# A fifth staging buffer, another order of stores and wider pieces in the background weight preparation of a fused attention and mixture-of-experts kernel

## The chip, the cores and the metric

The program runs on one core of one Trainium2 chip, as one launch. The metric is device time in microseconds: the median of several runs without the profiler. Beside it stands one profiled execution, whose trace gives the rows below.

## The reference, cut to what matters

```python
# x1 = attention(q, k, v): 4 x 8 heads, 576 positions, head size 64, causal window of 64,
#      laid out as 2304 tokens x 512
def _moe_ref(x, w_gate, w1, w2):            # dense: all 8 experts on all tokens
    P = np.exp(x @ w_gate - ...)            # then 8 rounds of row and column scaling
    for e in range(8):
        out += P[:, e:e+1] * (np.maximum(x @ w1[e], 0) @ w2[e])    # 512 -> 1024 -> 512
def _moe2_ref(x, w_gate, w1, w2):           # routed: each token goes to one expert, 288 per expert
    for e in range(8):
        mask = assigned == e
        out[mask] = np.maximum(x[mask] @ w1[e], 0) @ w2[e]
```

The output is `_moe2_ref(_moe_ref(attention))`, in float32.

## The kernel before

Matrix products with weights run in float16 with two halves: a float32 value is written as a high half and a low half, and three products (high-high, high-low, low-high) are summed in PSUM. The halves of a weight have to be made on the chip. ScalarE (ACT) makes the high half with one scaled copy and VectorE (DVE) makes the low half as the difference (`split_f`, lines 345 and 347). That pair is called a split here: 512 columns, 128 partitions.

The program has three parts. First, attention over 18 tiles of 128 tokens, together with the first expert of the dense layer; here the instruction order comes from a planner, `Flow`, with estimated costs, and the flag `bg.hold` is true. Second, experts 1 to 7 of the dense layer in a written-out order: `layer1s` and `layer2s` run one level of Strassen's scheme, seven products for each pair of token tiles, nine pairs for each expert. Third, the routed layer: `route`, `ffn` and `put`.

While the second part runs, `weights_all` prepares weights in the background, job after job. A job loads one float32 weight matrix (2 MB, in four quarters) into the one buffer `raw` (`load`, line 1621), computes its scale from sums of squares (`sum_scale`, line 287 on ACT, line 302 on TensorE), and makes splits. Each split goes into a buffer named `st2k`, of which there are 4, and from there by DMA into a scratch tensor in HBM, from which later stages load it: `w1scr` (`strassen_w1`, line 427, 14 splits), `w2scr` (`quarters_w2`, line 533, 14 splits, and `prep_w2`, line 498), `ws` for the routed layer (`prep_moe2`, line 473, 8 splits). These stores are issued by GpSimd (POOL). There are 31 jobs. When a quarter of `raw` is no longer needed, `free(r)` issues the load of the same quarter for the next job on SyncE (SP).

The pace of the background is counted in units. `layer1s` and `layer2s` call `bg.tick(0, DT / 2)` twice in each product, with DT = 1.4, so a product advances the background by 1.4 units. Before a split the job waits SPW units, and between its high and low half LOW = 0.7 units. After the load of a quarter is issued, its squares are not put into the instruction order before 11 units have passed (`bg.ready`). The order of instructions on each engine is fixed by this when the program is built; on the chip an engine that has to wait holds everything behind it.

In `strassen_w1` the seven outputs are made in the order A22, A11, A12, S1, S2, S3, S4, and then all four quarters of `raw` are freed. S4 is a sum written over A12 by DVE (line 414).

For expert 1 alone, `quarters_w2` runs during attention, with `bg.hold` true; its 14 splits use four slices of `acc` as buffers instead of `st2k`, and are stored by POOL as well. During attention SP also issues the loads of q, k and v for tiles ahead, and POOL also runs the reductions of `largest_v` over partitions.

In the last dense expert, `held_gate` uses a tile `xT2` for a transposed row block, and `rc["y"]` holds the scaled results that POOL adds into `acc` by DMA (line 1085).

Of the kernel before, what the change touches and what calls it, by code (L numbers as in the profile page):

```python
# [8 lines left out]
F32 = mybir.dt.float32  # L9
# [5 lines left out]
PSUM = bass.MemoryType.PSUM  # L15
M2PLAN = {1: 2, 2: 2, 3: 2, 4: 3, 5: 2, 6: 3, 7: 2}
DT = 1.4
SPW = 1.2
LOW = 0.7
MANE, MANP = 1, 1  # L20
PR = (4, 0)
# [154 lines left out]
def body(ctx, tc, dims, q, k, v, wg1, w11, w12, wg2, w21, w22, wgT, out):  # L176
# [154 lines left out]
    w2flat = [w2b[:, o:o + 4096] for o in (0, 4096)]  # L331
    w2v = [t.rearrange("p (c f) -> p c f", c=FC) for t in w2flat]

    def st2k():
        return rc["pool"].tile([128, 1040], F16, name="st2k", bufs=4)

    def wsc():
        return small.tile([128, 1], F32, name="wsc", bufs=3)
# [38 lines left out]
    def strassen_w1(e, sc, free):  # L377
        wr = raw.rearrange("p (c f) -> p c f", c=DC)
        hf = F // 2
        A11, A12 = wr[:, 0:2, 0:hf], wr[:, 2:4, 0:hf]  # L380
        A21, A22 = wr[:, 0:2, hf:], wr[:, 2:4, hf:]

        def sp(src, name):
            for c in range(2):
                yield from split_f(src[:, c], wq[name][0][:, c], wq[name][1][:, c], sc, 512, wait=1.2 if e == 1 else 1.8)

        if e == 1:
            t3 = acc[:, NT - 2:]

            def comb(dst, x, y, op):  # L390
                yield Rq("DVE", 1.2, wait=1.5)
                V.tensor_tensor(dst, x, y, op)

            yield from comb(t3, A11, A21, OP.subtract)
            yield from comb(A21, A21, A22, OP.add)
            while "T" not in rc:
                yield IDLE
            yield from sp(t3, "S3")
            yield from comb(t3, A21, A11, OP.subtract)
            yield from sp(t3, "S2")  # L400
            yield from comb(t3, A12, t3, OP.subtract)
            while ("l1", e - 1) not in bg.done:
                yield IDLE
            yield from sp(A21, "S1")
            yield from sp(A11, "A11")
            yield from sp(A12, "A12")
            yield from sp(A22, "A22")
            yield from sp(t3, "S4")
        else:
            t3 = rc["tmp"]  # L410

            def comb(dst, x, y, op):
                yield Rq("DVE", 1.2, wait=1.5)
                V.tensor_tensor(dst, x, y, op)

            def out(src, name):
                o = W1N.index(name) * 2048
                for c in range(2):
                    st = []

                    def two():
                        st.append(st2k()[:, 0:1024].rearrange("p (t x) -> p t x", t=2))
                        return st[0][:, 0], st[0][:, 1]

                    yield from split_f(src[:, c], two, None, sc, 512, wait=SPW)
                    d = w1scr[e * 128:(e + 1) * 128, o:o + 2048].rearrange("p (t x) -> p t x", t=2)
                    G.dma_start(d[:, :, c * 512:(c + 1) * 512], st[0])

            yield from comb(t3, A11, A21, OP.subtract)
            yield from out(A22, "A22")  # L430
            yield from comb(A21, A21, A22, OP.add)
            yield from out(A11, "A11")
            yield from comb(A11, A21, A11, OP.subtract)
            yield from out(A12, "A12")
            yield from comb(A12, A12, A11, OP.subtract)
            for n, q in ((A21, "S1"), (A11, "S2"), (t3, "S3"), (A12, "S4")):
                yield from out(n, q)
            bg.done.add(("w1p", e))
        for r in range(4):
            free(r)  # L440
        if e == 1:
            bg.done.add(("w1", e))

    W1N = ("A11", "A12", "S2", "S1", "S3", "S4", "A22")
# [15 lines left out]
    def prep_moe2(e, m, free):  # L460
        sc = wsc()
        yield from sum_scale(raw, winv[:, 2 + m, e:e + 1], sc, "job")
        for c in range(8):
            a, cc = (c % 2, c // 2) if m == 0 else (c // 4, c % 4)
            st = []

            def two():
                st.append(st2k()[:, 0:1024].rearrange("p (t x) -> p t x", t=2))
                return st[0][:, 0], st[0][:, 1]

            x, y = yield from split_f(raw[:, c * 512:(c + 1) * 512], two, None, sc, 512, pool="st2k", wait=SPW if c else 1.0)
            d = wscr[m][a][e * 128:(e + 1) * 128, :].rearrange("p (t x) -> p t x", t=2)
            G.dma_start(d[:, :, cc * 512:cc * 512 + 512], st[0])  # L473
            fl.release("st2k", x.idx, y.end + 4.6)
            if c % 2:
                free(c // 2)
# [7 lines left out]
    def w2rows(e):  # L484
        return w2scr[e * 128:(e + 1) * 128, 0:2 * FC * DM].rearrange("p (t x) -> p t x", t=2)

    def prep_w2(e, free):
        yield from sum_scale(raw, winv[:, 1, e:e + 1], w2sc, "job")
        for c in range(8):
            cs = slice(c * 512, (c + 1) * 512)  # L490
            st = []

            def two():
                st.append(st2k()[:, 0:1024].rearrange("p (t x) -> p t x", t=2))
                return st[0][:, 0], st[0][:, 1]

            x, y = yield from split_f(raw[:, cs], two, None, w2sc, 512, pool="st2k", wait=SPW if c else 1.0)
            G.dma_start(w2rows(e)[:, :, cs], st[0])
            fl.release("st2k", x.idx, y.end + 4.6)
            if c % 2:  # L500
                free(c // 2)
        bg.done.add(("w2p", e))

    def quarters_w2(e, free):
# [14 lines left out]
        def sp(src, name):  # L519
            o = QN.index(name) * 2048  # L520
            for c in range(2):
                st = []

                def two():
                    t = acc[:, 12 + cnt[0] % 4].bitcast(F16) if e == 1 else st2k()[:, 0:1024]
                    cnt[0] += 1
                    st.append(t.rearrange("p (t x) -> p t x", t=2))
                    return [st[0][:, n].rearrange("p (b x) -> p b x", x=hd) for n in range(2)]

                x, y = yield from split_f(src[:, 2 * c:2 * c + 2], two, None, w2sc, 512, deps=[("w2", 0)] if e == 1 else (),  # L530
                                          pool=None if e == 1 else "st2k", wait=SPW)
                d = w2scr[e * 128:(e + 1) * 128, o:o + 2048].rearrange("p (t x) -> p t x", t=2)
                G.dma_start(d[:, :, c * 512:(c + 1) * 512], st[0])  # L533
                fl.release("st2k", x.idx, y.end + 4.6)

        yield from comb(t3, B22, B12, OP.subtract)
# [532 lines left out]
    def layer2s(e, k):  # L1069
# [17 lines left out]
        def step(q):  # L1087
            def f():
# [10 lines left out]
                m = 0  # L1099
                for c in range(4):  # L1100
                    for hi, wi in ((0, 0), (0, 1), (1, 0)):
                        PE.matmul(bank[:, 0:hd], hq[hi][:, c], wv[wi][:, c], start=(pool is not None and m == 0), stop=(m == 11),  # L1102
                                  skip_group_check=True)
                        m += 1
                    if c % 2:
                        bg.tick(0, DT / 2)
# [395 lines left out]
    def ffn(ph, before, between):  # L1502

        xt, ws, idx, sv = PH[ph]
        hh, hl = [t[:, :, 0:CAP] for t in hbuf[ph % 2]]
        wv1 = [[ws[0][:, a * 4096 + o * 2048:a * 4096 + (o + 1) * 2048].rearrange("p (c f) -> p c f", c=DC)
                for o in range(2)] for a in range(2)]
        wv2 = [[ws[1][:, a * 4096 + o * 2048:a * 4096 + (o + 1) * 2048].rearrange("p (c f) -> p c f", c=FC // 2)
                for o in range(2)] for a in range(2)]
        for f in range(FC):  # L1510
            p = ps1.tile([128, 512], F32, name="p1")
            n = 0
# [103 lines left out]
    def load(k, r):  # L1616
        if k < len(jobs):
# [2 lines left out]
            n = src.shape[1] // 4  # L1620
            SP.dma_start(raw.rearrange("p (c f) -> p c f", c=src.shape[1])[:, r * n:(r + 1) * n], src[:, r * n:(r + 1) * n])
            fl.at["job", r] = fl.load(512)
            bg.ready["job", r] = bg.now + 11.0

    def weights_all():
        for r in range(4):
# [61 lines left out]
    def change():  # L1688
# [10 lines left out]
        rc["xr"] = mpool.tile([128, 3, 2 * XO], F16, name="xr")  # L1699
        w1x = mpool.tile([128, 6144], F16, name="w1x")  # L1700
        w2x = mpool.tile([128, 2048], F16, name="w2x")
        rc["xT2"] = mpool.tile([128, 512], F32, name="xT2")
        rc["y"] = mpool.tile([128, 2, DM], F32, name="y")
        slots = [w1b[:, o:o + 1024] for o in range(0, 8192, 1024)] + [w1x[:, o:o + 1024] for o in range(0, 6144, 1024)]
        for i, n in enumerate(("A12", "A22", "S1", "A11", "S3", "S2", "S4")):
            wq[n] = [t.rearrange("p (c f) -> p c f", c=2) for t in slots[2 * i:2 * i + 2]]
        rc["w1q"] = dict(zip(("A12", "A22", "S1", "A11", "S3", "S2", "S4"), [w1b[:, o:o + 2048] for o in range(0, 8192, 2048)]
                             + [w1x[:, o:o + 2048] for o in range(0, 6144, 2048)]))
        w2q = [w2b[:, o:o + 2048] for o in range(0, 8192, 2048)] + [hall[:, 7168:9216], hall[:, 9216:11264], w2x]
        rc["w2q"] = dict(zip(QN, w2q))  # L1710
        rc["w2v"] = {q: [t[:, o:o + 1024].rearrange("p (c x) -> p c x", c=4) for o in (0, 1024)] for q, t in zip(QN, w2q)}
        xhf = xh.rearrange("p c n -> p (c n)")
        xlf = xl.rearrange("p c n -> p (c n)")
        rc["hset"] = [hall[:, 0:7168], xhf[:, 0:7168]]
# [157 lines left out]
```

## Time and profile before

| | |
|---|---|
| median of 3 runs | 1818.23 us (1815.84 to 1824.08) |
| the profiled execution | 1835.57 us |
| its span, first to last instruction | 1833.8 us |
| mean granted TensorE clock | 0.987 |
| TensorE matmul busy | 1747.1 us, 95% of the span |
| VectorE, ScalarE, GpSimd busy | 1320.6, 1042.4, 421.9 us |

The profiled execution is 17.3 us longer than the median of the runs without a profile. Busy times are unions of an engine's instructions; TensorE's are modelled, since matmuls overlap. A waiting engine is idle in these counts. A view of waits names for each idle stretch the instruction or DMA that ended it.

### The profile page before, as it was taken

How to read it: one execution, taken by the hardware profiler on the slowest of the kernel's cores; microseconds unless marked ns; L12 is line 12 of the kernel's file. 1: busy time of each engine (PE TensorE's matmuls, PEld its weight loads, DVE VectorE, ACT ScalarE, POOL GpSimd, SP SyncE). 2: the span in 40 equal slices, each digit the busy share in tenths (PEclk: the TensorE clock that was granted, in tenths of full speed). 3: DMA queues.
4: the chain of work that ended last, by engine and by line, in shares of the span. 5: the costliest groups of instructions: out<-in, count | busy, mean ns of one | idle time of the engine just before them, and what ended most of it. 6: DMA issues, size and time to landing. Idle time of an engine off the chain costs nothing.

```text
span 1833.8 us, 51148 instructions
## 1 busy us (share of the span) xinstructions
PE 1747.1 (95%) x21427; PEld 1478.8 (81%) x21427; DVE 1320.6 (72%) x3136; ACT 1042.4 (57%) x2039; POOL 421.9 (23%) x566
## 2 busy tenths in 40 slices
PE   5999999999999999999999999999999997999988
PEld 4665557899899999999999999998887774677766
DVE  8888985787786787788678867876767757565630
ACT  6777254667677676767776767766654431222222
POOL 0011000233232232333233222322311111232231
PEclk9999999999999999999999999999999998899999
DMA  7454236669867786788688678976972202554360
GB/s 222 125 185 148 72 122 234 188 187 307 275 179 235 253 298 183 252 274 276 201 256 300 212 214 276 281 231 184 287 258 82 76 25 72 183 178 169 129 226 27
DMA packets 125079, 361.35 MB, mean 197 GB/s; under 512 B 15728, under 2 KB 27248, under 8 KB 120752
## 3 DMA queue, kind: packets, MB, share of 16 engines
q1 hardware_dynamic: 77296, 207.04, 34.0%
q0 software_dynamic: 47552, 151.04, 27.1%
q8 instruction: 168, 2.75, 0.6%
q14 instruction: 63, 0.52, 0.1%
HBM read 232.31 MB, written 97.40 MB: 180 GB/s over the span
## 4 chain that ended last, share of the span: by engine, by line
PE 58%; issue 15%; DVE 11%; DMA 9%; POOL 3%; ACT 3%; another core or an unknown queue 1%; POOLq 0%; SPq 0%; ACTq 0%; DVEq 0%
PE p L965 11%; PE p L1102 8%; PE pb L965 8%; PE pb L1102 5%; PE p L1530 5%; PE p L1130 4%; PE p L1152 4%; DMA ws<-st2k 4%; PE p L1516 3%; PE p L829 3%; DMA w2scr<-st2k 2%; PE pb L1361 1%; POOL acc L1085 1%; POOL w2scr L533 1%; DMA raw<-in_moe_w_dram 1%
## 5 line engine op out<-in xcount | busy, mean ns | idle before, releaser
L965 PEld LDWEIGHTS <-w1b 128*128 128x128 f16 x6048 | 361.1, 98 | 9.7 <-issue 0.7
L965 PEld LDWEIGHTS <-w1x 128*128 128x128 f16 x4536 | 269.4, 98 | 15.6 <-issue 8.0
L1102 PEld LDWEIGHTS <-xh 128*128 128x128 f16 x2268 | 215.8, 99 | 34.4 <-issue 9.2
L1102 PEld LDWEIGHTS <-hall 128*128 128x128 f16 x2268 | 214.8, 98 | 28.3 <-issue 4.0
L347 DVE SCALAR_TENSOR_TENSOR st2k<-raw,wsc,st2k 128x512 f16<-128x512 f32 x200 | 149.1, 749 | 67.6 <-ACT st2k L345 67.1
L965 PE MATMUL p<-xr,w1x 128*128 128x128 f16 x3024 | 189.7, 219 | 6.5 <-ACT xl L982 6.4
L965 PE MATMUL pb<-xr,w1b 128*128 128x128 f16 x3024 | 192.1, 220 | 0.0
L965 PE MATMUL p<-xr,w1b 128*128 128x128 f16 x3024 | 190.0, 219 | 0.4 <-DVE xl L985 0.4
L345 ACT ACTIVATE st2k<-raw,wsc 128x512 f16<-128x512 f32 x200 | 140.8, 714 | 75.7 <-DMA ws<-st2k 55.5
L1085 POOL DMA_DIRECT2D acc<-y x108 | 101.4, 939 | 265.8 <-ACT y L1083 248.0
L1083 ACT ACTIVATE y<-p,SE 128x256 f32<-128x256 f32 x216 | 101.2, 468 | 82.4 <-PE p L1102 78.0
L473 POOL DMA_DIRECT2D ws<-st2k x128 | 93.5, 733 | 222.8 <-DVE st2k L347 208.7
L985 DVE TENSOR_TENSOR xl<-pb,xl 128x512 f32<-128x512 f32 x126 | 86.7, 688 | 74.6 <-PE pb L965 69.0
L287 ACT ACTIVATE junk<-raw 128x1024 f16<-128x1024 f32 x108 | 113.4, 1050 | 11.4 <-DMA raw<-in_moe_w_dram 11.2
L1078 DVE SCALAR_TENSOR_TENSOR acc<-pb,SE,acc 128x256 f32<-128x256 f32 x162 | 77.9, 481 | 55.5 <-PE pb L1102 32.7
L829 PE MATMUL p<-xh,w1b 128*128 128x384 f16 (+1 forms) x512 | 101.4, 289 | 6.7 <-DVE hall L811 6.5
L533 POOL DMA_DIRECT2D w2scr<-st2k x70 | 52.5, 751 | 234.1 <-PE pb L965 122.1
L1130 PE MATMUL p<-w2b,hall 128*128 128x512 f16 x432 | 105.4, 379 | 0.0
L1152 PE MATMUL p<-w2b,hall 128*128 128x512 f16 x432 | 97.0, 379 | 0.0
L829 PEld LDWEIGHTS <-w1b 128*128 128x128 f16 x768 | 64.3, 100 | 38.2 <-issue 9.0
L965 PE MATMUL pb<-xr,w1x 128*128 128x128 f16 x1512 | 95.1, 219 | 0.0
L982 ACT ACTIVATE xl<-p 128x512 f32<-128x512 f32 x126 | 74.2, 589 | 35.5 <-PE p L965 35.5
(328 smaller groups left out, 3552.0 us busy)
## 6 DMA issues: line engine op xcount, KB each, us to landing
raw<-in_moe_w_dram SPq DMA_DIRECT2D x128, 512.0 KB, 5.8
xr<-xtd SPq DMA_DIRECT2D x63, 896.0 KB, 6.5
ws<-st2k POOLq DMA_DIRECT2D x128, 256.0 KB
acc<-y POOLq DMA_DIRECT2D x108, 256.0 KB
w1scr<-st2k POOLq DMA_DIRECT2D x84, 256.0 KB
w2scr<-st2k POOLq DMA_DIRECT2D x78, 256.0 KB
w2b<-w2scr SPq DMA_DIRECT2D x28, 512.0 KB, 6.5
w1b<-w1scr SPq DMA_DIRECT2D x24, 512.0 KB, 9.0
```

What stands on the lines that cost most here:

```text
L287: A.activation(rc["junk"], buf[:, c * 1024:(c + 1) * 1024], AF.Square, accum_out=mp[:, c:c + 1])
L345: A.activation(hi, src, AF.Copy, scale=sc)
L347: V.scalar_tensor_tensor(lo, src, sc, hi, op0=OP.mult, op1=OP.subtract)
L473: G.dma_start(d[:, :, cc * 512:cc * 512 + 512], st[0])
L829: PE.matmul(p[:, 0:w], w1v[wi][:, c, fs], x[:, c, ts], start=(n == 0), stop=(n == 3 * DC - 1))
L965: PE.matmul(bank[:, fs], aq[wi][:, c, fs], xq[xi][:, c], start=(start and f == 0 and m == 0), stop=(m == 5), skip_group_check=True)
L1083: A.activation(y[:, h * hd:(h + 1) * hd], bank[:, 0:hd], AF.Copy, scale=SE[:, e, i:i + 1])
L1085: G.dma_start(acc[:, i], y, accum_op=OP.add)
L1102: PE.matmul(bank[:, 0:hd], hq[hi][:, c], wv[wi][:, c], start=(pool is not None and m == 0), stop=(m == 11), skip_group_check=True)
L1130: PE.matmul(s[0], h[hi].rearrange("p (c t) -> p c t", c=4)[:, f % 4], w2v[wi][:, f], start=(f == 0 and hi == wi == 0), stop=(f == FC - 1 a ...
L1152: PE.matmul(p, h[:, f, js], w2v[wi][:, f], start=(n == 0), stop=(n == 3 * FC - 1))
L1530: PE.matmul(p[:, 0:CAP], wv2[f // 4][w][:, f % 4, dsl], x[:, f], start=(n == 0), stop=(n == 3 * FC - 1))
```

## The change

- The buffer count of `st2k` goes from 4 to 5. The planner's own count, `Flow({... "st2k": 4})`, stays.
- SPW goes from 1.2 to 1.1 units, and the 11 units after a load's issue become 13.
- In the scratches of w1, of the quartered w2 and of the routed layer the high and the low half of one split now lie side by side: one split is one run of 2 KB for each partition in HBM, where it was two runs of 1 KB. The views with which the matmuls read the loaded weights are adapted. `prep_w2` keeps its two runs.
- A new function `store` issues the stores: by SP while `bg.hold` is true, else by POOL as before.
- In `strassen_w1` for experts 2 to 7 the order becomes A22, A11, A12, S4, S1, S2, S3; quarters 2 and 3 of `raw` are freed after S4, quarters 0 and 1 after S2.
- `xT2` loses its own tile and becomes the second half of `y`.

```diff
-SPW = 1.2
+SPW = 1.1
...
+    def store(dst, src):
+        (SP if bg.hold else G).dma_start(dst, src)
+
     def st2k():
-        return rc["pool"].tile([128, 1040], F16, name="st2k", bufs=4)
+        return rc["pool"].tile([128, 1040], F16, name="st2k", bufs=5)
...
                     def two():
-                        st.append(st2k()[:, 0:1024].rearrange("p (t x) -> p t x", t=2))
-                        return st[0][:, 0], st[0][:, 1]
+                        st.append(st2k()[:, 0:1024])
+                        return st[0][:, 0:512], st[0][:, 512:1024]
 
                     yield from split_f(src[:, c], two, None, sc, 512, wait=SPW)
-                    d = w1scr[e * 128:(e + 1) * 128, o:o + 2048].rearrange("p (t x) -> p t x", t=2)
-                    G.dma_start(d[:, :, c * 512:(c + 1) * 512], st[0])
+                    store(w1scr[e * 128:(e + 1) * 128, o + c * 1024:o + c * 1024 + 1024], st[0])
...
             yield from comb(A12, A12, A11, OP.subtract)
-            for n, q in ((A21, "S1"), (A11, "S2"), (t3, "S3"), (A12, "S4")):
-                yield from out(n, q)
+            yield from out(A12, "S4")
+            for r in (2, 3):
+                free(r)
+            yield from out(A21, "S1")
+            yield from out(A11, "S2")
+            for r in (0, 1):
+                free(r)
+            yield from out(t3, "S3")
             bg.done.add(("w1p", e))
-        for r in range(4):
-            free(r)
         if e == 1:
+            for r in range(4):
+                free(r)
             bg.done.add(("w1", e))
...
-            d = wscr[m][a][e * 128:(e + 1) * 128, :].rearrange("p (t x) -> p t x", t=2)
-            G.dma_start(d[:, :, cc * 512:cc * 512 + 512], st[0])
+            store(wscr[m][a][e * 128:(e + 1) * 128, cc * 1024:cc * 1024 + 1024], st[0])
...
-            G.dma_start(w2rows(e)[:, :, cs], st[0])
+            store(w2rows(e)[:, :, cs], st[0])
...
-                d = w2scr[e * 128:(e + 1) * 128, o:o + 2048].rearrange("p (t x) -> p t x", t=2)
-                G.dma_start(d[:, :, c * 512:(c + 1) * 512], st[0])
+                store(w2scr[e * 128:(e + 1) * 128, o + c * 1024:o + c * 1024 + 1024], st[0])
...
-            bg.ready["job", r] = bg.now + 11.0
+            bg.ready["job", r] = bg.now + 13.0
...
-        rc["xT2"] = mpool.tile([128, 512], F32, name="xT2")
         rc["y"] = mpool.tile([128, 2, DM], F32, name="y")
+        rc["xT2"] = rc["y"][:, 1]
```

## Rows read from the trace of the kernel before

**Rows 1.** Each stage: us, busy (instructions) per engine, granted clock, DMA share, GB/s.
```profile
120.00:200.00 80.00, 75.44 (x785) 46.45 (x783) 69.57 (x248) 49.63 (x159) 12.64 (x20) 1.00 0.39 128
...
300.00:1350.00 1050.00, 1025.12 (x13794) 967.97 (x13792) 799.56 (x1268) 725.43 (x1211) 303.70 (x393) 0.99 0.77 243
```

**Rows 2.** TensorE's waits in 300 to 1350: total us, times, longest us.
```profile
PE p L1102 <- ACT y L1083: 8.9, 7, 2.8
PE p L965 <- ACT xl L982: 6.4, 7, 2.2
PE pb L1102 <- DVE acc L1078: 2.6, 5, 0.7
...
PE pb L302 <- ACT junk L287: 2.1, 1, 2.1
```

**Rows 3.** ScalarE's waits in 300 to 1365, those ended by a DMA.
```profile
ACT st2k L345 <- DMA ws<-st2k: 55.5, 31, 4.6
...
ACT st2k L345 <- DMA w2scr<-st2k: 31.9, 26, 4.0
...
ACT st2k L345 <- DMA w1scr<-st2k: 13.8, 12, 2.5
...
ACT junk L287 <- DMA raw<-in_moe_w_dram: 11.2, 6, 4.3
```

**Rows 4.** ScalarE in order of time around one of those waits.
```profile
612.07 0.72 ACT L345 ACTIVATE st2k<-raw,wsc 128x512 f16<-128x512 f32 x1 [3.77 <-DMA ws<-st2k]
```

**Rows 5.** GpSimd's stores in the same stretch, in order of time.
```profile
601.88 0.71 POOL L473 DMA_DIRECT2D ws<-st2k  x1 [6.38 <-DVE st2k L347]
604.66 0.72 POOL L473 DMA_DIRECT2D ws<-st2k  x1 [2.08 <-DVE st2k L347]
```

**Rows 6.** The chain of work that ended last, one of its pieces there: start, us.
```profile
606.82 10.50 DMA ws<-st2k
```

**Rows 7.** Stretches with a lowered mean clock (first, last of four), columns as in rows 1.
```profile
320.00:360.00 40.00, 36.62 (x473) 34.41 (x472) 27.71 (x44) 25.43 (x44) 10.26 (x13) 0.96 0.66 206
...
1240.00:1280.00 40.00, 37.82 (x494) 35.20 (x492) 26.44 (x46) 26.00 (x44) 9.26 (x12) 0.96 0.66 193
```

**Rows 8.** TensorE in order of time behind its idle stretch at 465.6.
```profile
467.63 0.39 PE L302 MATMUL pb<-np,ones 128*128 128x4 f32 x2 [2.06 <-ACT junk L287]
...
469.40 2.77 PE L1102 MATMUL p<-w2x,xh 128*128 128x256 f16 x12
...
473.52 1.47 PE L1102 MATMUL p<-w2b,hall 128*128 128x256 f16 x12
```

**Rows 9.** ScalarE, SyncE and GpSimd, 160 to 180, each in order of time.
```profile
170.82 0.72 ACT L345 ACTIVATE acc<-raw,w2sc 128x512 f16<-128x512 f32 x1 [5.25 <-DMA w2scr<-acc]
...
163.48 15.20 SPq L1621 DMA_DIRECT2D raw<-in_moe_w_dram  x4
...
163.94 3.01 POOL L533 DMA_DIRECT2D w2scr<-acc  x4 [3.33 <-ACT acc L345]
```

**Rows 10.** TensorE in order of time, its two idle stretches there.
```profile
172.56 0.32 PE L829 MATMUL p<-xh,w1b 128*128 128x384 f16 x1 [2.17 <-DVE hall L811]
...
176.70 0.63 PE L686 MATMUL pb<-ident,pn 128*128 128x128 f32 x4 [2.03 <-DVE pn L638]
```

**Rows 11.** The chain again: one product of 24 matmuls.
```profile
360.78 1.34 PE p L965 x24
```

**Rows 12.** VectorE in order of time: the sum that makes S4.
```profile
374.20 1.23 DVE L414 TENSOR_TENSOR raw<-raw 128x1024 f32<-128x1024 f32 x1
```

**Rows 13.** Two stretches with many splits and stores, columns as in rows 1.
```profile
1160.00:1200.00 40.00, 40.00 (x548) 37.98 (x546) 35.92 (x56) 28.34 (x47) 14.09 (x19) 1.00 0.88 269
...
480.00:500.00 20.00, 20.00 (x279) 19.03 (x278) 18.30 (x27) 13.30 (x21) 8.66 (x12) 1.00 1.01 331
```

**Rows 14.** VectorE and TensorE in time order: held weights' last product, first use.
```profile
1462.70 0.69 DVE L1235 SCALAR_TENSOR_TENSOR y<-raw,st2k 128x512 f16<-128x512 f32 x1
...
1503.15 0.35 PE L1261 MATMUL pb<-w2h,hall 128*128 128x16 f16 x8
```

More of the change, by code (lines that the diff above doesn't have):

```diff
@@ L467, in two @@
             def two():
-                st.append(st2k()[:, 0:1024].rearrange("p (t x) -> p t x", t=2))
-                return st[0][:, 0], st[0][:, 1]
+                st.append(st2k()[:, 0:1024])
+                return st[0][:, 0:512], st[0][:, 512:1024]
             x, y = yield from split_f(raw[:, c * 512:(c + 1) * 512], two, None, sc, 512, pool="st2k", wait=SPW if c else 1.0)
-            d = wscr[m][a][e * 128:(e + 1) * 128, :].rearrange("p (t x) -> p t x", t=2)
-            G.dma_start(d[:, :, cc * 512:cc * 512 + 512], st[0])
+            store(wscr[m][a][e * 128:(e + 1) * 128, cc * 1024:cc * 1024 + 1024], st[0])
             fl.release("st2k", x.idx, y.end + 4.6)
@@ L526, in two @@
                     cnt[0] += 1
-                    st.append(t.rearrange("p (t x) -> p t x", t=2))
-                    return [st[0][:, n].rearrange("p (b x) -> p b x", x=hd) for n in range(2)]
+                    st.append(t)
+                    return [t[:, n * 512:n * 512 + 512].rearrange("p (b x) -> p b x", x=hd) for n in range(2)]
                 x, y = yield from split_f(src[:, 2 * c:2 * c + 2], two, None, w2sc, 512, deps=[("w2", 0)] if e == 1 else (),
                                           pool=None if e == 1 else "st2k", wait=SPW)
-                d = w2scr[e * 128:(e + 1) * 128, o:o + 2048].rearrange("p (t x) -> p t x", t=2)
-                G.dma_start(d[:, :, c * 512:(c + 1) * 512], st[0])
+                store(w2scr[e * 128:(e + 1) * 128, o + c * 1024:o + c * 1024 + 1024], st[0])
                 fl.release("st2k", x.idx, y.end + 4.6)
@@ L1101, in f @@
                     for hi, wi in ((0, 0), (0, 1), (1, 0)):
-                        PE.matmul(bank[:, 0:hd], hq[hi][:, c], wv[wi][:, c], start=(pool is not None and m == 0), stop=(m == 11),
+                        PE.matmul(bank[:, 0:hd], hq[hi][:, c], wv[wi][c], start=(pool is not None and m == 0), stop=(m == 11),
                                   skip_group_check=True)
@@ L1505, in ffn @@
         hh, hl = [t[:, :, 0:CAP] for t in hbuf[ph % 2]]
[L1506 to L1509, printed above, removed]
+        wv1, wv2 = [[[v[:, o] for o in range(2)] for v in
+                     [w[:, a * 4096:(a + 1) * 4096].rearrange("p (c t f) -> p t c f", c=4, t=2) for a in range(2)]] for w in ws]
         for f in range(FC):
@@ L1701, in change @@
         w2x = mpool.tile([128, 2048], F16, name="w2x")
-        rc["xT2"] = mpool.tile([128, 512], F32, name="xT2")
         rc["y"] = mpool.tile([128, 2, DM], F32, name="y")
-        slots = [w1b[:, o:o + 1024] for o in range(0, 8192, 1024)] + [w1x[:, o:o + 1024] for o in range(0, 6144, 1024)]
-        for i, n in enumerate(("A12", "A22", "S1", "A11", "S3", "S2", "S4")):
-            wq[n] = [t.rearrange("p (c f) -> p c f", c=2) for t in slots[2 * i:2 * i + 2]]
+        rc["xT2"] = rc["y"][:, 1]
         rc["w1q"] = dict(zip(("A12", "A22", "S1", "A11", "S3", "S2", "S4"), [w1b[:, o:o + 2048] for o in range(0, 8192, 2048)]
                              + [w1x[:, o:o + 2048] for o in range(0, 6144, 2048)]))
+        for n, t in rc["w1q"].items():
+            v = t.rearrange("p (c t f) -> p t c f", c=2, t=2)
+            wq[n] = [v[:, 0], v[:, 1]]
         w2q = [w2b[:, o:o + 2048] for o in range(0, 8192, 2048)] + [hall[:, 7168:9216], hall[:, 9216:11264], w2x]
         rc["w2q"] = dict(zip(QN, w2q))
-        rc["w2v"] = {q: [t[:, o:o + 1024].rearrange("p (c x) -> p c x", c=4) for o in (0, 1024)] for q, t in zip(QN, w2q)}
+        rc["w2v"] = {q: [[t[:, a * 1024 + o * 512 + c * 256:a * 1024 + o * 512 + c * 256 + 256] for a in range(2)
+                          for c in range(2)] for o in range(2)] for q, t in zip(QN, w2q)}
         xhf = xh.rearrange("p c n -> p (c n)")
```

## The prediction, made before the change was run

> **What bounds the kernel now.** I read first the busy time of each stage, to see which engine could give time back. In the long stage of experts 1 to 7, from 300 to 1350 us, TensorE is busy 1025.1 of 1050 us [rows 1], and a product of 24 matmuls takes 1.34 us [rows 11], 56 ns for each. The change takes no matmul away. So this stage can give back only the 24.9 us in which TensorE is idle, and what a lowered clock costs behind such stretches. Before it, between 120 and 200 us, another 4.6 us are idle [rows 1].
>
> Then I read who ends TensorE's idle stretches. Nearly three quarters of the time is late emptying of PSUM: 8.9 + 6.4 + 2.6 = 17.9 us in 19 stretches wait for ACT or DVE to read a bank; one stretch of 2.1 us waits for the sums of squares [rows 2]. The reader is to see next why ACT is late: its waits name the store of an earlier split, 55.5 + 31.9 + 13.8 = 101.2 us in 69 waits, 1.5 us on average, at most 4.6 [rows 3]. All four `st2k` buffers are then still being stored, ACT's split stands in front, and the emptying of PSUM is queued behind it. That makes 17.9 / 101.2 = 0.18 us of idle TensorE for 1 us of ACT's wait, an upper ratio, since a few of the 19 stretches have other reasons. The chain of work shows the same: a piece "DMA ws<-st2k" of 10.5 us [rows 6].
>
> Third, the clock. In four stretches of 40 us the mean granted clock is 0.96 [rows 7], so for a part of them TensorE runs at the lower of its two levels, 1.2 instead of 2.4 GHz. One row shows it: right behind an idle stretch of 2.06 us, 12 matmuls take 2.77 us, where 1.47 us is usual [rows 8]. A mean of 0.96 costs 0.04 x 40 = 1.6 us, four times 6.4 us. Three of the four lie around store waits (the first and the last of [rows 7] among them), one around the raw load [rows 8].
>
> **The fifth buffer.** How long a buffer is bound shows in one place. The split that ACT starts at 612.07 waited 3.77 us [rows 4]; it takes the buffer whose store POOL issued at 604.66, so the data landed some 7.4 us after the issue. With five buffers it would take the one of the store before, issued at 601.88, 2.78 us earlier [rows 5]; at equal delay 1.0 us of wait is left. By pace: a product is 1.4 units and 1.34 us, a unit 0.96 us. Four splits at 1.2 + 0.7 units last 7.3 us, five at 1.1 + 0.7 last 8.6, so cover grows by 1.3 us at least, against a mean wait of 1.5. Bounds: nothing, if the stores fall behind as fast as ACT runs ahead; 17.9 us of idle time and 4.8 us of clock, if every wait goes. I take 12 of 17.9 and 3 of 4.8, since the one place worked out keeps a quarter of its wait: **-15 us**.
>
> **Load slack (11 to 13 units).** ACT waits 11.2 us for `raw` in 6 waits, at most 4.3 [rows 3]; 2 units are 1.9 us. The longest of them made the 2.06 us gap and its slow clock, 2.06 + 1.6 = 3.7 us. Between 0 and 3.7 I take **-2**.
>
> **Stores by SP in attention.** This touches only the 14 splits of expert 1 in `acc` slices. Now four of them are issued in a row from 163.94, behind loads of `raw` that SP had started at 163.48; ACT waits 5.25 us for one [rows 9] and TensorE is idle 2.17 and 2.03 us [rows 10]. After the change store and load stand in one SP queue in program order, and the two stores of T1 come before the load, so that they move first. Bounds 0 and 4.2; I take **-2.5**. The Trainium skill ("DMA: Bandwidth & Descriptors", section "Issuing engines are not separate DMA queues") says that DMAs started by any engine share the same 16 engines and that another issuer saves only issue time. By that this term would be 0 and the forecast 2.5 us higher; I keep the row, because here the order against the load changes too. What is queued behind each such store on SP: loads of q, k, v for later tiles. POOL's part gets shorter, and the reductions on it no longer stand behind stores.
>
> **Two pieces of 1 KB become one of 2 KB.** Bytes, number of stores and number of splits stay. No row shows what a store of 2 KB pieces gains; the split's two halves lie side by side in SBUF already. Between nothing and the same 101.2 us of waits that the fifth buffer attacks, I take 0, as it can only win what is already counted.
>
> **S4 in fourth place.** Its split now directly follows the sum that makes A12, 1.23 us on DVE [rows 12]; the split is put 1.1 units, 1.05 us, behind it. So ACT may wait up to about 1.2 us, in six jobs, 7.2 us, at 0.18: **+1.3 us**, between 0 and that. In return the loads for the next job start during the last splits, quarters 2 and 3 six splits ahead of the end, 0 and 1 two. Then those stores share the DMA with 2 MB of loads, as those of w2 do now. w2's 26 waits cost 31.9 us and w1's 12 only 13.8 [rows 3], so with four buffers this would be 18 us x 0.18 = 3.3 us; with five I take **+0.7**.
>
> **Pace of the background.** A job of 14 splits gets shorter by 1.4 units, one of 8 by 0.7. The later gate of loads adds 2 units to a job whose predecessor frees its last quarter at its end; behind a w1 job it takes away 1.6, since the first quarters are now freed 3.6 units ahead (13 - 3.6 = 9.4 against 11). For an expert with one w2, one w1 and two routed jobs: 3 x 2 - 1.6 - 2 x 1.4 - 2 x 0.7 = +0.2 units; over all experts, with those of three routed jobs, some 7 units, 7 us later. Cover: held weights read `raw` last at 1462.70 and their result is first used at 1503.15 [rows 14], 40 us. Cost 0. The denser splits meet a DVE that is busy 35.92 of 40 us at worst, while TensorE there is at 40.00 of 40 [rows 13]; I add **+1** for both. `xT2` in `y` can make a copy wait for an adding DMA once: between 0 and some 2 us, **+0.3**.
>
> **Sum.** -15 - 2 - 2.5 + 1.3 + 0.7 + 1 + 0.3 = -16.2 us against the profiled execution's 1835.6, which gives 1819.4. The median without a profile is 17.3 us lower; taken over in proportion, 16.2 x 1818.2 / 1835.6 = 16.0, the forecast is **1802 us**. About 0.5%, 9 us, is what a measurement of this kernel can tell from no change.
>
> **The rivals.**
> *The transfers limit, not the buffers (0.14).* For: the DMA engines' share is 1.01 between 480 and 500 us [rows 13], in the middle of a burst of stores. A fifth buffer then only moves the wait by one split, and the quicker pace makes the queue longer. Against: over the whole stage the share is 0.77 [rows 1], and bursts have 8 or 14 splits, so one buffer more is a good part of a burst. With 4 of the 15 us, the rest as above: 1835.6 - 5.2, or 1813.
> *The waits are smaller without the profile (0.14).* For: the profiled execution is 17.3 us longer than the median. If half of that were such waits, 9 of the 19.5 gained us would not be there to win: some 1811. Against: nothing in the trace shows where the 17.3 us lie.
> *VectorE becomes the bound in bursts (0.07).* For: 35.92 of 40 us in [rows 13]. A split every 1.72 instead of 1.82 us adds 6% to its part of that work, and without ACT's waits more work moves together. Should DVE need 105% of the time in some 24 bursts of 25 us, TensorE would lose 24 x 1.25 = 30 us, and the time would be 1832, slower. It decides from the point where 40 of 40 us are reached; that is 11% away, and in that stretch TensorE has no idle time at all, which is against it.
> *The forecast (0.62)*, with a range of its own from 1791 to 1809; 0.03 is left for what I don't see.
>
> **How the numbers follow.** The low end takes all terms at their best: 17.9 + 4.8 + 3.7 + 4.2 = 30.6, so about 1788; I stop at 1790. The high end takes in the second and the third case: 1818. Faster by over 0.5% (below 1809): nearly all of the forecast and a quarter of the two middle cases, 0.66; within: 0.25; slower: 0.09.
>
> **What the profile after would show.** Right: ACT's waits for stores of `st2k` fall from 101 us to below 35; TensorE's waits for ACT's and DVE's reading of banks fall from 17.9 to about 6; fewer of the four stretches at 0.96; the wait of 5.25 us near 170 is gone; ACT's waits for `raw` fall below 6 us. Wrong: the store waits stay above 60 us at the same DMA share (first rival); they vanish and the time does not move (second); TensorE's idle time changes its releaser to DVE (third). Longer waits of attention's scores for q or k would show that SP's stores stand in the way.

## The result and the profile after

The changed kernel takes 1798.13 us, the median of five runs (1795.53 to 1799.21); the kernel before took 1820.91 us beside it (1815.84 to 1824.08). The ratio is 0.9876, with a 95% interval from 0.9856 to 0.9896: 1.2% faster, 22.8 us between the medians. The forecast was 1802 us, -16 us.

The page of the changed kernel, span, busy time and TensorE's clock in 40 slices:

```profile
span 1793.7 us, 51089 instructions
...
PE 1736.8 (97%) x21427; PEld 1475.6 (82%) x21427; DVE 1319.6 (74%) x3136; ACT 1045.2 (58%) x2039; POOL 362.4 (20%) x552
...
PEclk9999999999999999999999999999999999899999
```

The two profiled spans, 1833.8 and 1793.7 us, are 40 us apart, the medians 23; the first experiment shows where most of the difference lies. TensorE has the same 21427 matmuls. The first product of expert 1 starts at 288.60 us instead of 291.27, and the first product with the held weights (line 1267, [rows 14] for before) comes 1187.82 instead of 1211.88 us behind it. So in this pair of profiles 2.7 us come from attention and 24.1 from experts 1 to 7. Two more profiles of the changed kernel have 1191.80 and 1191.49 us for experts 1 to 7, a second one of the kernel before 1211.70, so that stage gains 20 to 24 us. The stages, columns as in [rows 1]:

```profile
120.00:200.00 80.00, 78.64 (x804) 48.33 (x803) 72.64 (x260) 51.21 (x162) 2.64 (x6) 1.00 0.39 128
...
300.00:1350.00 1050.00, 1040.52 (x14079) 983.57 (x14077) 811.69 (x1296) 738.36 (x1231) 257.14 (x398) 1.00 0.78 247
```

TensorE's idle time in the same 1050 us falls from 24.9 to 9.5 us, and the clock's mean is 1.00. GpSimd is busy 47 us less there. TensorE's waits from 290 to 1330 us, against [rows 2]:

```profile
PE pb L971 <- ACT xl L988: 4.8, 3, 2.0
PE p L1108 <- DVE hall L1049: 2.5, 1, 2.5
PE p L1108 <- ACT y L1089: 1.4, 2, 0.9
PE pb L302 <- ACT junk L287: 0.4, 1, 0.4
PE p L971 <- ACT xl L988: 0.2, 1, 0.2
PE p L971 <- DVE xl L991: 0.2, 1, 0.2
```

Late reading of banks, 17.9 us before, is 6.4 us now (4.8, 1.4 and 0.2), and the 4.8 belong to three places. ScalarE's waits from 290 to 1345 us, against [rows 3]:

```profile
ACT st2k L348 <- DMA ws<-st2k: 22.3, 14, 3.9
...
ACT st2k L348 <- DMA w1scr<-st2k: 13.5, 10, 3.9
ACT junk L287 <- DMA raw<-in_moe_w_dram: 11.0, 8, 3.3
ACT st2k L348 <- DMA w2scr<-st2k: 7.0, 7, 2.4
ACT st2k L348 <- DVE raw L417: 4.9, 5, 1.3
```

Waits for stores fall from 101.2 us (69) to 42.8 (31): those of w2 and of the routed layer shrink, those of w1 stay. The last row is new; it is the split of S4 waiting for the sum that makes S4. The two stretches of [rows 7], which stood at 0.96, in the changed kernel:

```profile
320.00:360.00 40.00, 39.81 (x542) 37.64 (x541) 32.51 (x51) 28.95 (x49) 10.35 (x16) 1.00 0.67 203
1240.00:1280.00 40.00, 40.00 (x546) 37.97 (x544) 29.76 (x48) 30.15 (x50) 10.46 (x16) 1.00 0.77 237
```

In this profile no stretch of 40 us between 280 and 1320 is below 1.00 any more. The two other profiles of the changed kernel have one each, at 0.96, from 680 to 720. The same wait stands there in all three. TensorE in order of time, first this profile, then the second:

```profile
700.38 1.50 PE L971 MATMUL pb<-xr,w1x 128*128 128x128 f16 x24 [2.00 <-ACT xl L988]
701.72 1.47 PE L1108 MATMUL pb<-hall 128*128 128x256 f16 x12
```

```profile
703.29 2.28 PE L971 MATMUL pb<-xr,w1x 128*128 128x128 f16 x24 [2.06 <-ACT xl L988]
705.37 2.38 PE L1108 MATMUL pb<-hall 128*128 128x256 f16 x12
```

So an idle stretch of 2 us brings the lower clock in one execution and not in another.

In attention, ScalarE and SyncE around the place of [rows 9]:

```profile
166.32 0.72 ACT L348 ACTIVATE acc<-raw,w2sc 128x512 f16<-128x512 f32 x1
...
164.16 1.02 SPq L335 DMA_DIRECT2D w2scr<-acc  x2
165.23 2.49 SPq L1625 DMA_DIRECT2D raw<-in_moe_w_dram  x2
167.82 8.21 SPq L335 DMA_DIRECT2D w2scr<-acc  x4
```

Two stores now stand before the loads of `raw`. They land a median 3.0 us after their issue, and the split in `acc` waits for nothing, where it waited 5.25 us. Of TensorE's two idle stretches, 2.17 and 2.03 us, one of 1.01 is left.

### The profile page after: what moved, and what is told of

The parts are those of the page before. It is cut to its first block, busy times and chain, and to the rows that moved or that the text cites. A ratio compares the mean times of both kernels' runs of the same rounds, so it can differ in the third digit from the quotient of the medians.

```text
span 1793.7 us, 51089 instructions
## 1 busy us (share of the span) xinstructions
PE 1736.8 (97%) x21427; PEld 1475.6 (82%) x21427; DVE 1319.6 (74%) x3136; ACT 1045.2 (58%) x2039; POOL 362.4 (20%) x552
## 5 line engine op out<-in xcount | busy, mean ns | idle before, releaser
L1091 POOL DMA_DIRECT2D acc<-y x108 | 95.8, 887 | 327.1 <-ACT y L1089 292.6
L287 ACT ACTIVATE junk<-raw 128x1024 f16<-128x1024 f32 x108 | 113.2, 1049 | 11.2 <-DMA raw<-in_moe_w_dram 11.0
L335 POOL DMA_DIRECT2D ws<-st2k x128 | 73.5, 576 | 191.9 <-DVE st2k L350 184.1
L335 POOL DMA_DIRECT2D w2scr<-st2k x78 | 46.4, 594 | 242.2 <-DVE st2k L350 236.3
```

Of the source, the lines that this page charges most:

```text
L287: A.activation(rc["junk"], buf[:, c * 1024:(c + 1) * 1024], AF.Square, accum_out=mp[:, c:c + 1])
L335: (SP if bg.hold else G).dma_start(dst, src)
L1091: G.dma_start(acc[:, i], y, accum_op=OP.add)
```

## The experiments

Theory A: the fifth buffer takes away ACT's waits, and with them TensorE's; the rest of the change is small. Rival B: the wider pieces make stores land sooner. Rival C: pace and order of the background make the gain. All ratios are to the kernel before on the same chip, in 4 to 12 runs of each kernel.

**The kernel before, profiled again.** No edit.

> The kernel before, unchanged, profiled a second time. The 40 us between the two profiled spans fall into 2.7 us up to the first product of expert 1, 24.1 us in experts 1 to 7 and 13.3 us behind them, in the routed stage, on whose instructions the change has hardly any bearing. Theory A (the 13.3 us belong to that one execution): this second profile shows a routed stage of 317 to 322 us and a span near 1820, with the expert stage still near 1212 and its waits for stores near 101 us. Rival (they belong to the kernel before): the routed stage is again near 330 us and the span near 1833.

Ratio 1.0001 (0.9988 to 1.0014); the second span is 1820.4 us. Two stretches of this profile, the expert stage as in [rows 1] and the routed stage:

```profile
300.00:1350.00 1050.00, 1023.93 (x13799) 967.01 (x13797) 798.67 (x1267) 725.45 (x1211) 303.61 (x393) 1.00 0.77 243
...
1520.00:1820.40 300.40, 278.21 (x2846) 206.34 (x2843) 163.73 (x646) 72.09 (x149) 76.21 (x80) 0.96 0.43 149
```

This is what theory A said. The expert stage repeats (26.1 us idle, 24.9 before; waits for stores 100.6 us), but three stretches of 40 us stand at 0.96 where the first profile had four, and only two of them in the same places. The routed stage, behind the first product with held weights, is 13.8 us shorter than in the first profile, 316.9 against 330.6 us. So most of the surplus of the first profile over the median was that stage of one execution, and no part of the change.

**The changed kernel with four buffers.**

```diff
-        return rc["pool"].tile([128, 1040], F16, name="st2k", bufs=5)
+        return rc["pool"].tile([128, 1040], F16, name="st2k", bufs=4)
```

> The changed kernel with 4 buffers for st2k instead of 5; all else stays. Theory A (buffers): most of the gain goes, 1811 to 1820 us, ACT's waits for stores are back at 100 us or more, since the pace is denser and w1's loads now meet its stores; TensorE's idle time in the expert stage is back near 25 us. Rival B (the wider pieces make the stores land sooner, POOL's issue fell from some 710 to 580 ns): 1798 to 1804 us and waits near 50 us. Rival C (pace and order of loads): the same as B.

1820.94 us, ratio 1.0005 (0.9990 to 1.0019): the whole gain is gone. ScalarE's and TensorE's waits in it:

```profile
ACT st2k L348 <- DMA ws<-st2k: 62.0, 38, 4.3
ACT st2k L348 <- DMA w2scr<-st2k: 30.9, 22, 3.2
ACT st2k L348 <- DMA w1scr<-st2k: 21.7, 14, 4.1
...
PE p L971 <- ACT xl L988: 13.2, 9, 4.7
PE p L1108 <- ACT y L1089: 8.5, 7, 1.9
```

Waits for stores are 114.6 us, more than the 101.2 before, and TensorE is idle 28.6 us from 300 to 1350. Nothing else in the change makes up for the buffer; B and C fall as sole causes.

**The kernel before with five buffers alone.**

```diff
-        return rc["pool"].tile([128, 1040], F16, name="st2k", bufs=4)
+        return rc["pool"].tile([128, 1040], F16, name="st2k", bufs=5)
-        rc["xT2"] = mpool.tile([128, 512], F32, name="xT2")
+        rc["xT2"] = rc["y"][:, 1]
```

> The kernel before with a fifth buffer alone (and with xT2 in y, which makes room for it). Theory A (buffers): 1802 to 1808 us, ACT's waits for stores fall from 101 us to 20 to 40. Rival B (wider pieces) and rival C (pace and order): 1815 to 1822 us, with waits above 70 us.

1803.11 us, ratio 0.9893 (0.9877 to 0.9909), as theory A said. The waits that are left in it:

```profile
ACT junk L287 <- DMA raw<-in_moe_w_dram: 28.6, 16, 5.3
ACT st2k L345 <- DMA ws<-st2k: 13.9, 11, 2.3
ACT st2k L345 <- DMA w2scr<-st2k: 11.6, 11, 3.2
...
PE pb L302 <- ACT junk L287: 6.2, 5, 1.8
```

Waits for stores are 25.5 us, none for w1. Now `raw` is late: with the splits no longer held up, ACT reaches the squares before the load has landed, 28.6 us where it was 11.2, and TensorE waits 6.2 us for their sums, where it was 2.1 [rows 2, 3]. That is the stall next in line, and what the 13 units meet.

**The old layout in the changed kernel**, run twice, the second time beside the changed kernel itself. Each store and each view of loaded weights goes back to two runs of 1 KB; of the four places one is shown:

```diff
-            store(wscr[m][a][e * 128:(e + 1) * 128, cc * 1024:cc * 1024 + 1024], st[0])
+            d = wscr[m][a][e * 128:(e + 1) * 128, :].rearrange("p (t x) -> p t x", t=2)
+            store(d[:, :, cc * 512:cc * 512 + 512], st[0])
```

> The changed kernel with the old layout of the scratches: each split is stored as two runs of 1 KB again, and the matmuls read the weights as before. Theory A (buffers): 1797 to 1801 us, no change that can be told; POOL's issue time returns to 700 ns, which is hidden. Rival B (wider pieces): 1806 to 1815 us, ACT's waits for stores clearly above 50 us, and a longer time from issue to landing.

> The changed kernel with the old layout, as run before, now on the same chip as the changed kernel itself. Theory A (the layout does nothing to the time): within 2 us of the changed kernel. Rival (the wider pieces cost some 4 us, as the ratios 0.9845 and 0.9876 say): 3 to 6 us below the changed kernel.

> The changed kernel unchanged, the base for the kernel with the old layout on the same chip: ratio 0.987 to 0.989 as twice before.

1793.85 us, ratio 0.9845 (0.9831 to 0.9860), and 1794.60, 0.9851 (0.9834 to 0.9869). The changed kernel beside the second: 1798.46, 0.9876 (0.9858 to 0.9895). The old layout is 3.9 us faster in medians on one chip, where the rival of the second run said 3 to 6; the first run is faster than either side said. The intervals overlap by 0.0011; the results on other chips, 0.9876 and 0.9877 for the changed kernel and 0.9845 for the old layout, stand the same way. GpSimd's store issues, changed kernel:

```profile
L335 POOL DMA_DIRECT2D ws<-st2k x128 | 73.5, 576 | 191.9 <-DVE st2k L350 184.1 <-issue 4.0 <-DVE xl L991 2.4
```

and with the old layout:

```profile
L335 POOL DMA_DIRECT2D ws<-st2k x128 | 93.5, 736 | 178.3 <-DVE st2k L350 171.0 <-ACT st2k L348 3.1 <-DVE xh L1061 2.3
```

The wider pieces save POOL 160 ns for each store, but POOL is idle before them for 191.9 us in all, 184.1 of it waiting for DVE, and the median from issue to landing is no shorter (6.4 to 6.7 us for the routed weights in three profiles, against 6.2 in both with the old layout). B is refuted. Of the loss, 2.2 us lie at the very end: behind the last matmul of `ffn` the span runs on for 10.7 us in three profiles of the changed kernel and for 8.5 in both with the old layout. The pieces alone don't set this: the kernel before, with 1 KB pieces, has 9.6 there, and the changed kernel with all stores by GpSimd, with 2 KB pieces, 12.0. What makes that end longer stays open, and so does whether the pieces cost the rest.

**All stores by GpSimd.**

```diff
-        (SP if bg.hold else G).dma_start(dst, src)
+        G.dma_start(dst, src)
```

> The changed kernel with all stores by POOL again, also the 14 of expert 1 during attention. Theory A (store before load in one SP queue): the time up to the first product of expert 1 returns from 288.6 to 291 to 292 us, the wait of some 5 us near 170 us is back, 1800 to 1802 us in all. Rival (the wider pieces of these 14 stores, or other order in attention, make the 3 us): the first stage stays at 288 to 289 us and the time at 1798.

1803.75 us, ratio 0.9892 (0.9869 to 0.9916), beside 1799.53, 0.9877 (0.9855 to 0.9900), for the changed kernel on the same chip. The first product of expert 1 is at 293.3 us, where the changed kernel has 288.4 to 289.4 in three profiles, and two idle stretches of 1.6 and 2.0 us at 171 and 175 us are back. Both the stage and the time are a little above what theory A said. The stores that POOL issues there beside SP's loads of `raw` land 6.2 to 6.7 us after issue, against 3.0 for the two that stand ahead of the loads in SP's queue. The gain in attention is SP's stores, 4.2 us by medians, though the intervals overlap.

> The changed kernel unchanged, as a base on the same chip, and a second profile. Theory A (the old layout was some 4 us faster, 0.9845 against 0.9876, which is not chance): ratio 0.987 to 0.989 here too. Rival (difference between chips): 0.984 to 0.986.

The ratio of 0.9877 is what theory A said: a difference between chips is not what sets the old layout apart.

**S4 last again.**

```diff
-            yield from out(A12, "S4")
-            for r in (2, 3):
-                free(r)
             yield from out(A21, "S1")
             yield from out(A11, "S2")
-            for r in (0, 1):
-                free(r)
             yield from out(t3, "S3")
+            yield from out(A12, "S4")
+            for r in range(4):
+                free(r)
```

> The changed kernel with S4 as the last sum of w1 again and all four quarters freed at the end, as before. Theory A (the early loads of raw collide with w1's last stores, which the forecast put at 0.7 us): the idle stretches of 2.0, 1.9 and 0.9 us that end with ACT's reading of a bank behind waits for w1scr stores go, w1's store waits fall from 13.5 to below 3 us; waits for raw may rise from 11 to some 20 us; 1794 to 1799 us. Rival (the early loads are what keeps waits for raw short, and the order pays): waits for raw above 25 us, TensorE idle 5 us more, 1801 to 1806 us.

1807.94 us, ratio 0.9934 (0.9910 to 0.9959), some 8 us slower than the changed kernel. Neither side had it right. The collision goes, w1's store waits fall to 1.8 us, and waits for `raw` are 11.9 us, no longer than in the changed kernel. But the background is later: its last split of `raw` starts at 1375.4 us instead of 1339.5 (the last time in each row, of the view of the tile `st2k`), first this kernel, then the changed one:

```profile
L348 ACT ACTIVATE st2k<-raw,wsc x200: 705/712/723, 354.7 to 1375.4; 128x512 f16<-128x512 f32 x100
```

```profile
L348 ACT ACTIVATE st2k<-raw,wsc x200: 705/712/732, 354.3 to 1339.5; 128x512 f16<-128x512 f32 x100
```

With S4 last it runs into the row stores of the last expert, which use `st2k` too. One of its splits waits there for such a store, and TensorE is idle for 4.45 us:

```profile
1367.33 0.72 ACT L348 ACTIVATE st2k<-raw,wsc 128x512 f16<-128x512 f32 x1 [7.68 <-DMA xrows<-st2k]
```

**11 units instead of 13.**

```diff
-            bg.ready["job", r] = bg.now + 13.0
+            bg.ready["job", r] = bg.now + 11.0
```

> The changed kernel with 11 units instead of 13 behind a load's issue. Theory A (as in the kernel with the fifth buffer alone, where ACT waited 28.6 us for raw and TensorE 6.2 us for the sums of squares): waits for raw rise from 11 to 25 to 30 us, TensorE's for the sums from 0.4 to some 5 us, 1802 to 1805 us. Rival (with early loads the slack is there already): 1797 to 1799 us, waits for raw below 15 us.

1819.47 us, ratio 0.9992 (0.9979 to 1.0006): this too undoes the whole gain, far more than theory A's 1802 to 1805. The waits in it:

```profile
PE pb L302 <- ACT junk L287: 5.6, 3, 3.2
PE pb L971 <- ACT xl L988: 4.5, 2, 2.5
PE p L1108 <- ACT y L1089: 4.3, 2, 3.3
...
ACT junk L287 <- DMA raw<-in_moe_w_dram: 26.6, 14, 5.2
ACT st2k L348 <- DMA w1scr<-st2k: 24.9, 13, 4.7
```

Waits for `raw` are what was expected, but w1's stores are waited for 24.9 us as well, where the kernel with the fifth buffer alone had none. That kernel has 11 units too, and its waits for `raw` are longer, yet it takes 1803.11 us: 11 units are dear only together with something else that the change brings. Four stretches of 40 us are at 0.96 again. Three lie behind waits of 3.6 to 4.7 us for w1's stores, the longest of which ScalarE and TensorE show so:

```profile
843.75 0.72 ACT L348 ACTIVATE st2k<-tmp,wsc 128x512 f16<-128x512 f32 x1 [4.68 <-DMA w1scr<-st2k]
...
844.88 2.72 PE L1108 MATMUL p<-hall,xh 128*128 128x256 f16 x12 [3.34 <-ACT y L1089]
```

The fourth lies behind the longest wait for the sums:

```profile
480.00:520.00 40.00, 36.78 (x478) 34.27 (x476) 29.93 (x47) 23.89 (x40) 8.50 (x13) 0.96 0.65 217
```

The background's last split of `raw` starts at 1296.2 us, 43 us sooner than in the changed kernel.

**15 units, and the slower pace, both with the old layout.**

```diff
-            bg.ready["job", r] = bg.now + 13.0
+            bg.ready["job", r] = bg.now + 15.0
```

> The changed kernel with the old layout and 15 units behind a load's issue instead of 13. Theory A (more slack takes away what is left of the waits for raw, some 10 us, worth 1 to 2 us; but each job gets longer by up to 2 units, some 50 us in all over the background): waits for raw below 4 us, the last splits run into the last expert's row stores, 1796 to 1806 us. Rival (slack is all): 1788 to 1793 us.

1822.84 us, ratio 1.0003 (0.9984 to 1.0022), slower than either side said. Waits for `raw` fall to 3.9 us as expected, but the last split is at 1407.6 us, and the held weights come too late. TensorE waits for them, and then routing is no longer hidden behind other products:

```profile
1505.08 0.36 PE L1270 MATMUL pb<-w2h,hall 128*128 128x16 f16 x8 [3.78 <-DVE w2h L1258]
...
1520.00:1560.00 40.00, 19.84 (x269) 14.13 (x266) 26.53 (x99) 3.52 (x7) 7.50 (x7) 0.57 0.37 132
```

In that stretch TensorE is busy half the time, and the granted clock falls to 0.57; with 13 units and the old layout the same stretch has 31.61 us and 0.79.

```diff
-SPW = 1.1
+SPW = 1.2
```

> The changed kernel with the old layout (two runs of 1 KB) and with SPW = 1.2, so that the pace of the splits is that of before; 13 units, S4 in fourth place, five buffers and SP's stores stay. Theory A (buffers and load slack make the gain, the pace little; a slower pace eases the collision of w1's stores with the early loads): 1790 to 1796 us, w1's store waits below 10 us. Rival (the pace is needed, since a later background runs into the last expert's row stores, as with S4 last): 1800 to 1808 us, last split of the background later than 1350 us.

1795.91 us, ratio 0.9861 (0.9844 to 0.9878): with 13 units and the early loads the pace of the splits makes no difference that can be told. Store waits are lower (28.5 us against 41.2 and 42.0 with 1.1), but w1's stay at 11.0. The last split is at 1369.2 us, nearly as late as with S4 last, and waits 1.23 us for a row store there: a late end alone does not cost the 8 us. Theory A's time was right, its reason about w1 not.

## Why the prediction held, and where it was off

The forecast was 16 us, and 22.8 were measured. The cause named for most of it was right. That the rest came so near is in part luck: the terms beside the buffer sum to -1.2 us, and the whole change is 3 to 5 us below the buffer alone (0.9876 against 0.9893; the intervals overlap), but taken out one by one, order, slack and SP's stores are worth 8, 20 and 4 us.

**The bound and the fifth buffer: right.** The gain is TensorE's idle time and its busy time for the same matmuls in attention and the expert stage; the routed stage has 316.9 us in the second profile of before and 317.3 in that of the change. The buffer alone gives 1.07% (0.91 to 1.23), 19.5 us by the ratio and 17.9 between the medians, with a forecast of 15, and without it nothing is left. Store waits fell to 42.8 us, not below 35: the early loads keep w1's at 13.5, while the buffer alone reached 25.5. The rival by which the transfers limit would have left them above 60; the DMA share is 0.78, where it was 0.77.

**The clock and the idle time: both under-sized.** Without attention's 2.5, the forecast for experts 1 to 7 was 13.7 us; between the first product of expert 1 and the first with held weights, two profiles of the kernel before and three of the changed one give 19.9 to 24.1. Of these, 13.2 to 16.3 are idle time and 5.5 to 9.0 are busy time for the same matmuls, where I took 12 and 3, and 2 of both for the slack. Stretches at 0.96 fell from four and three to none, one and one, which at 1.6 us each makes 3.2 to 6.4 us. The last 2 to 3 us of busy time don't show in the clock's means, and what they are stays open.

**Load slack: mis-sized, and no term of its own.** I gave the 13 units 2 us and said that the waits for `raw` would fall below 6 us; they are 11.0, as before. Taken away from the changed kernel the units are worth 20 us (1819.47 against 1799.53). One mistake was to read the waits for `raw` from the kernel before: there the store waits themselves gave the loads time, and with the buffer free 11.2 us of waits became 28.6. But this alone costs little, as the kernel before with the fifth buffer shows, which takes 1803.11 us at 11 units. The larger mistake was to add up the terms as if each stood alone. Slack and order go together: with the old order and 13 units the time is 1807.94 us, with the new order and 11 units 1819.47, with both old 1803.11, with both new 1798 to 1800. The kernel with both old also has the old pace, layout and stores in attention, so that this is read across the runs, and no single run shows it.

**Stores by SP in attention: right.** 2.5 us forecast, 2.7 by the first profiles (1.9 to 3.5 over all pairs of them), 4.2 by the run with POOL. By the Trainium skill ("DMA: Bandwidth & Descriptors", section "Issuing engines are not separate DMA queues") this would have been the issue time alone. The traces disagree here: ahead of 1 MB of loads in SP's queue the two stores land in 3.0 us, and from POOL beside the loads in 6.2 to 6.7. At 158 us, where no load of `raw` is under way, one such store lands in 2.0 us from SP and in 2.3 from POOL, so it is the loads beside it that make the difference.

**S4 in fourth place: its price right, its worth missed.** The split of S4 waits 4.9 us for its sum in five places, with a bound of 7.2. The early loads make one idle stretch of TensorE behind a wait for w1's stores, 2.00 us at 700.38, more than the 0.7 us I gave them; the two others of that row, 1.92 and 0.87 us, lie behind waits for stores of the routed layer. What I counted at nothing was the gain: at 13 units the background ends 36 us sooner than with S4 last, and the order is worth some 8 us there, of which 4.45 are one wait for a row store.

**Pace and cover: right.** I had the background some 7 us later, out of 40 us of cover. Held weights read `raw` last at 1444.3 and are first used at 1476.4 us, so cover went from 40.4 to 32.1 us, by 8.3. The run with 15 units shows what happens when it is used up.

**Wider pieces: 0 forecast, some 4 us lost by medians.** More than half of it lies at the end of the span, and no run shows its cause.

**The other rivals.** VectorE did not become the bound: TensorE's idle stretches that end with DVE fell from 7.6 to 2.7 us between 300 and 1350. The rival by which the waits were smaller without a profile falls with the second profile of before: 100.6 us of store waits in an execution of 1822.16 us, the median of its runs.

## What to carry to other kernels

When one stall is removed, the stall behind it must be sized with the first one gone: a wait for a full buffer had been giving the loads their time. In a schedule written out in fixed units, each change of order asks for the units again: 11 units were within some 5 us of the changed kernel with the old order, cost 20 us with the early loads, and 15 units (with the old layout) used up the cover. So a change of order is tried with the unit on both sides of its value. The best version measured is the changed kernel with the old two runs of 1 KB: 1793.85 and 1794.60 us, ratios 0.9845 and 0.9851 to the kernel before.

## What the runs showed of the hardware

Pieces of 2 KB instead of 1 KB shortened the issue of a store by GpSimd from 736 to 576 ns and made neither the time to landing shorter (6.2 and 6.4 us) nor the kernel's time. Two stores of 256 KB ahead of 1 MB of loads in SP's queue landed 3.0 us after issue; stores from GpSimd, beside the loads, 6.2 to 6.7. An idle stretch of 2 us on TensorE can cost more than itself, and need not: behind one of 2.06 us, 24 and 12 matmuls took 2.28 and 2.38 us, and behind one of 2.00 us, at the same place of the same kernel, 1.50 and 1.47. Over the expert stage, 13.2 to 16.3 us less idle time came with 5.5 to 9.0 us less busy time for the same matmuls. The granted clock fell to a mean of 0.57 where TensorE was busy 19.84 of 40 us.
